# Three products of a chunked linear attention in column tiles of 32, in one stretch on TensorE, with the next unit's key transposes behind them

## The chip, the cores and the metric

One core of one Trainium2 chip runs the whole program. The time is device microseconds from launch to end; lower is better. Beside the timed runs there is one execution taken with the hardware profiler. All rows below are from that one.

## What is computed

A linear attention with a decaying state feeds two MLPs in a row. Four batches, eight heads, 768 steps, head size 48; then 3072 tokens through 384 → 2048 → 384 twice.

```python
for t in range(S):
    cur = np.einsum('bhd,bhe->bhde', u[None] * kt, vt)
    y[:, :, t] = np.einsum('bhd,bhde->bhe', rt, state + cur)
    state = wt[:, :, :, None] * state + np.einsum('bhd,bhe->bhde', kt, vt)
...
h = x @ w_in
g = np.where(h > 0.0, h, alpha * (np.exp(np.minimum(h, 0.0)) - 1.0))
return (g @ w_out).astype(np.float32)      # second MLP: g = h * sigmoid(h)
```

## The kernel before

The steps are cut into six chunks of 128. A **unit** is one chunk of one batch with all eight heads, that is, four pairs of heads; there are 24 units, numbered chunk by chunk (unit n is chunk n // 4 of batch n % 4). The first MLP works on six blocks of four units each. Block 0's units (0 to 3) are computed alone at the start (`dense_units`). From then on the attention of the next four units is woven into the first MLP of the present block: units 4 to 7 into block 0, and so on to units 20 to 23 into block 4. Block 5 and the whole second MLP have no attention beside them.

A block has 16 **slots**, one for each 128 of the 2048 hidden channels. A slot issues nine wide matmuls into `ph` (L447), then nine into `po` (L478) for the slot two before it, and calls `tick` twice, once behind each nine. A tick takes at most one of the six steps `t0` to `t5` of a unit (`round_ticks`), so a unit is spread over some seven ticks. Every engine runs its instructions in program order.

The steps of unit n on TensorE: `scores` (L274 for units below 9, L282 from there on) in t0 and t1, the key transposes `ktok` (L300) in t3, `past` (L345: the state against the decayed queries) and `outer` (L315: keys against values, for the state) in t4, `within` (L365: the masked scores against values) in t5. Around them: `masked` on VectorE (L291), which reads the score buffers; `ktok_copy` on ScalarE (L306), which brings the transposed keys to SBUF for `outer`; `update` (VectorE L325 and L327, then two copies on ScalarE, L329), which brings the product of `outer` into the state; `split` (ScalarE L377 `xh`, then VectorE L378 `xl`), which brings `y`, the sum of `past` and `within`, into the MLP's input. The same steps also prepare unit n + 1 (`do(...)`): decay scans, the products q and k with their decays (`q`, `kt`), the bonus diagonal (`diag`). Units 4 and 8 (`ALONE`) are prepared at the head of their block (`prep_rest`).

`past` writes `y`, 384 rows in three groups of 128 partitions, by seven matmuls 96, 32 or 64 columns wide; `outer` takes two per pair, 64 and 48 wide. `within` already writes tiles of 32 partitions only, four of them after one another on four different column groups. Units 20 to 23 are of the last chunk and have neither transposes nor `outer` nor `update`; units 0 to 3 are of the first and have no `past`.

Scores, transposes, `y`, the product of `outer` and the sums for the diagonal (L229) share three PSUM buffers (`ps_a`, tag `att`). A buffer is free again when the last instruction that reads it is done.

Of the kernel before, what the change touches and what calls it, by code (L numbers as in the profile page):

```python
# [7 lines left out]
F32 = mybir.dt.float32  # L8
# [5 lines left out]
ACTF = mybir.ActivationFunctionType  # L14
# [10 lines left out]
ALONE = (sum(BLOCKS[:1]), sum(BLOCKS[:2]))  # L25
# [9 lines left out]
def kernel(  # L35
# [21 lines left out]
    nc = tc.nc  # L57
    B, H, S, D = r.shape
    NT, DM = out.shape
    DFF = moe_w_out.shape[0]  # L60
    RB = w_ch.shape[2]
    L = 128
    NCH = S // L
    NU = B * NCH
    NP = H // 2
    KT = DM // 128
# [9 lines left out]
    ps_a = ctx.enter_context(tc.tile_pool(name="ps_a", bufs=3, space=PSUM))  # L76
# [4 lines left out]
    ch_p = attn.enter_context(tc.tile_pool(name="ch", bufs=2))  # L81
# [23 lines left out]
    ident = const.tile([128, 128], F32, name="ident")  # L105
# [28 lines left out]
    HALF = (slice(0, 64), slice(64, RB))  # L134
# [17 lines left out]
    def prep_steps(n):  # L152

        st = un[n]
# [87 lines left out]
        def kt():  # L242
            tk = st["kd"] = ch_p.tile([RB, NP, L], F32, tag="tk", name="tk")
            nc.vector.tensor_tensor(out=tk, in0=st["c"][:, 1], in1=k_decay, op=ALU.mult)
            if n >= FIRST_ROUNDED:
                rounding(tk, rounded["kh"], rounded["kl"])

        return dict(scan=scan, scan_back=scan_back, far=far, whole_decay=whole_decay, bonus=bonus, products=products, summed=summed, diag=diag,
                    q=q, kt=kt)


    state = [st_p.tile([RB, NP, 2 * D], F32, name=f"state{b}") for b in range(B)]
# [3 lines left out]
    def pe_steps(n, xt, col, free=None):  # L256
        ch, b = divmod(n, B)
        st = un[n]
        ps = {}

        def ps_att(shape, name):
            if free and name == "sc":
                return free.pop(0).rearrange("p (j t) -> p j t", j=NP)
            return ps_a.tile(shape, F32, tag="att", name=name)


        def scores(h):
            if n < FIRST_ROUNDED:

                if h == 0:  # L270
                    ps["p"] = [ps_att([128, NP, L], "sc") for _ in range(2)]
                for j in (2 * h, 2 * h + 1):
                    for e, rows in enumerate(HALF):
                        nc.tensor.matmul(  # L274
                            ps["p"][e][:, j, :], st["kd"][rows, j, :], st["q"][rows, j, :], start=True, stop=True)
                return
            p = ps["p", h] = ps_att([128, 2, 2, L], "sc")
            terms = [(rounded["k" + a], rounded["q" + b]) for a, b in ("hh", "hl", "lh")]
            for jj in range(2):
                j = 2 * h + jj  # L280
                for i, (a, b) in enumerate(terms):
                    nc.tensor.matmul(  # L282
                        p[:, jj].rearrange("p e t -> p (e t)"), a[:, j, :],
                        b[:, j].rearrange("p e t -> p (e t)"), start=i == 0, stop=i == len(terms) - 1)

        def masked(h):
            if n < FIRST_ROUNDED:
                to, p = st["a"][:, :, h, :], ps["p"][h]
            else:
                to, p = (t.rearrange("p j e t -> p (j e) t") for t in (st["a"][:, 2 * h:2 * h + 2], ps["p", h]))  # L290
            nc.vector.copy_predicated(to, upper.unsqueeze(1).to_broadcast([128, NP, L]), p)  # L291

        last = ch == NCH - 1

        def ktok():
            if last:
                return
            p = ps["kt"] = ps_att([128, NP, RB], "ktp")
            for j in range(NP):
                nc.tensor.transpose(p[:, j, :], st["kd"][:, j, :], ident[0:RB, 0:RB])  # L300

        def ktok_copy():
            if last:
                return
            t = st["kt"] = ch_p.tile([128, NP, RB], F32, tag="kt", name="kt", bufs=1)
            nc.scalar.activation(out=t, in_=ps["kt"], func=ACTF.Copy)  # L306

        def outer():
            if last:
                return  # L310
            p = ps["u"] = ps_att([RB, NP, D], "upd")
            for j in range(NP):

                for e, rows in enumerate(HALF):
                    nc.tensor.matmul(  # L315
                        p[rows, j, :], st["kt"][:, j, rows], st["v"][:, j, 64 * e:64 * e + D],
                        start=True, stop=True)

        def update():
            if last:  # L320
                return
            s, up = packed[b], ps["u"]
            g = st["gl"].to_broadcast([RB, NP, D])
            if ch:
                nc.vector.tensor_tensor(out=s, in0=up, in1=s, op=ALU.add)  # L325
                up = s
            nc.vector.tensor_tensor(out=s, in0=up, in1=g, op=ALU.mult)  # L327
            for e, rows in enumerate(HEAD):
                nc.scalar.activation(out=state[b][rows, :, e * D:(e + 1) * D], in_=s[rows], func=ACTF.Copy)  # L329

        def past():

            y = ps["y"] = ps_att([128, KT, L], "y")
            if not ch:
                return

            for j in range(NP):
                c0 = 2 * D * j
                while c0 < 2 * D * (j + 1):
                    kt, p0 = divmod(c0, 128)  # L340
                    m = min(2 * D * (j + 1) - c0, 128 - p0)
                    if p0 % 64:
                        m = 32
                    c = c0 - 2 * D * j
                    nc.tensor.matmul(  # L345
                        y[p0:p0 + m, kt, :], state[b][:, j, c:c + m], st["q"][:, j, :],
                        start=kt == 0, stop=False, skip_group_check=True)
                    c0 += m

        def within():  # L350
            y = ps["y"]
            vf = st["v"].rearrange("p j c -> p (j c)")
            for step in range(4):
                for base in range(4):


                    todo = []
                    for kt in range(KT):
                        blk = 4 * kt + base
                        j, i = divmod(blk, 3)  # L360
                        ha, hb = (64 + D) * j, (64 + D) * j + 64
                        todo += {0: [(blk, 2 * j, ha)], 1: [(blk, 2 * j, ha + 32), (blk, 2 * j + 1, hb - 16)],
                                 2: [(blk, 2 * j + 1, hb + 16)]}[i]
                    blk, h, c = todo[step]
                    nc.tensor.matmul(  # L365
                        y[32 * base:32 * base + 32, blk // 4, :], vf[:, c:c + 32], st["a"][:, h // 2, h % 2, :],
                        start=not ch and step == 0, stop=step == 3 or todo[step + 1][0] != blk,
                        skip_group_check=True)

        def split():  # L370
            split_x(xt, slice(col, col + L), ps["y"], nc.vector)

        return dict(scores=scores, masked=masked, ktok=ktok, ktok_copy=ktok_copy, outer=outer,
                    update=update, past=past, within=within, split=split)

    def split_x(xt, sl, src, eng):
# [177 lines left out]
    def round_ticks(n):  # L554
        pe, do = round_parts(n)

        def t0():
            pe["scores"](0)
            do("bonus")
            do("products")  # L560
            do("scan")
            load_unit(n + 2, "kr")

        def t1():
            pe["scores"](1)
            do("scan_back")
            do("whole_decay")
            if n + 1 not in ALONE:
                load_unit(n + 3, "w")
            pe["masked"](0)  # L570

        def t2():
            pe["masked"](1)
            do("summed")
            do("far")
            do("q")
            do("diag")

        def t3():
            pe["ktok"]()  # L580
            pe["ktok_copy"]()
            do("kt")
            do("diag", 1)
            if n + 1 not in ALONE:
                load_unit(n + 3, "c")

        def t4():
            pe["past"]()
            pe["outer"]()
            pe["update"]()  # L590

        def t5():
            pe["within"]()
            pe["split"]()
            load_unit(n + 2, "v")

        return [t0, t1, t2, t3, t4, t5]

    def dense_units():

        count = BLOCKS[0]
        prep, pe = {}, {}
# [5 lines left out]
        def begin(n):  # L608
            pe[n], _ = round_parts(n, [banks[3 * (n % 2)], banks[3 * (n % 2) + 1]])
            pe[n]["scores"](0)  # L610
            pe[n]["scores"](1)
            pe[n]["ktok"]()

        def keep_clock(k):
            for _ in range(k):
# [2 lines left out]
        for n in range(-1, count):  # L618
# [33 lines left out]
            if more:  # L652
                w_split()
                w_load()
                if n >= 0:
                    w_scale()
                pe[n + 1]["ktok_copy"]()
                p["diag"](0)
                p["diag"](1)
            if n == -1:  # L660
# [30 lines left out]
    last = None  # L691
# [299 lines left out]
```

## Time and profile before

| | |
|---|---|
| median of 3 timed runs | 966.77 us (966.73 to 966.84) |
| the profiled execution, its own time | 965.98 us |
| its span, first to last instruction | 964.1 us |
| TensorE busy in the span | 940.4 us (98%) |
| VectorE, ScalarE, GpSimd busy | 489.2, 501.4, 133.0 us |
| mean granted TensorE clock | 0.986 of full |
| share of the DMA engines' time, data packets | 22.3% |

A start in a timeline row is in us from the start of the span. TensorE starts matmuls while earlier ones still drain, so what one costs is read from one start to the next, not from its duration.

### The profile page before, as it was taken

What the parts mean: (1) busy time and instruction counts of PE and PEld (TensorE: products, weight loads), DVE (VectorE), ACT (ScalarE), POOL (GpSimd) and SP (SyncE); (2) the same over time, 40 slices, a digit from 0 to 9 for tenths busy, and PEclk for the clock granted to TensorE, in tenths of its full rate; (3) what the DMA queues carried; (4) which work ended last, traced back from release to release, by engine and by line L of the source; (5) the groups of instructions that cost most, each with busy time, mean ns of one, the idle gap of its engine ahead of it and who ended that gap; (6) DMA issues with size and microseconds to landing.
All of it is one profiled execution on the core that took longest, in us unless ns stands there. A gap on an engine that the chain in (4) does not pass through costs nothing.

```text
span 964.1 us, 14152 instructions
## 1 busy us (share of the span) xinstructions
PE 940.4 (98%) x5638; PEld 795.4 (82%) x5638; DVE 489.2 (51%) x726; ACT 501.4 (52%) x901; POOL 133.0 (14%) x101
## 2 busy tenths in 40 slices
PE   7779999999999999999999999999999999999997
PEld 7657777888778888887788889999999999999996
DVE  8789877766666666666357873212212212222111
ACT  6888857465555555465369884323323323333322
POOL 0000013343444333336000000000000000000000
PEclk8789999999999999999999999999999999999999
DMA  8644504211312222120054440010200200200001
GB/s 247 193 148 157 167 29 133 65 56 56 107 56 81 82 63 65 55 78 11 18 179 145 168 146 1 7 60 1 65 2 1 66 1 1 66 1 1 33 0 37
DMA packets 32218, 68.62 MB, mean 71 GB/s; under 512 B 3600, under 2 KB 13968, under 8 KB 32144
## 3 DMA queue, kind: packets, MB, share of 16 engines
q1 hardware_dynamic: 32144, 67.64, 22.3%
q8 instruction: 46, 0.75, 0.3%
q14 instruction: 28, 0.23, 0.1%
HBM read 58.19 MB, written 9.44 MB: 70 GB/s over the span
## 4 chain that ended last, share of the span: by engine, by line
PE 88%; ACT 4%; DVE 4%; issue 1%; ACTq 0%; DVEq 0%
PE ph L447 39%; PE po L486 21%; PE po L478 19%; PE y L345 3%; PE sc L282 2%; PE y L365 2%; ACT am L201 1%; ACT wh L432 1%; PE upd L315 1%; DVE wst L418 1%; ACT wst L409 1%; PE ktp L300 1%; DVE both L160 1%; DVE wst L420 1%; ACT am L178 0%
## 5 line engine op out<-in xcount | busy, mean ns | idle before, releaser
L470 DVE TENSOR_TENSOR gl<-g,gh 128x512 fp32r<-128x512 f32 x192 | 143.1, 745 | 319.7 <-ACT gh L469 318.9
L447 PE MATMUL ph<-xh,wh 128*128 128x512 f32 x576 | 229.6, 399 | 0.0
L447 PE MATMUL ph<-xl,wh 128*128 128x512 f32 x576 | 227.3, 395 | 0.0
L447 PE MATMUL ph<-xh,wl 128*128 128x512 f32 x576 | 227.2, 394 | 0.0
L469 ACT ACTIVATE gh<-g 128x512 fp32r<-128x512 f32 x192 | 120.9, 630 | 153.5 <-PE po L486 109.6
L486 PE MATMUL po<-wh,gl 128*128 128x384 f32 x384 | 129.6, 338 | 0.0
L486 PE MATMUL po<-wh,gh 128*128 128x384 f32 x384 | 129.4, 337 | 0.0
L458 ACT ACTIVATE g<-ph 128x512 f32<-128x512 f32 x96 | 57.3, 597 | 138.1 <-PE ph L447 137.3
L486 PE MATMUL po<-wl,gh 128*128 128x384 f32 x384 | 129.1, 336 | 0.0
L447 PEld LDWEIGHTS ph<-xh,wl 128*128 128x128 f32 x576 | 108.7, 189 | 23.5
L447 PEld LDWEIGHTS ph<-xh,wh 128*128 128x128 f32 x576 | 108.8, 189 | 21.8 <-issue 2.0
L447 PEld LDWEIGHTS ph<-xl,wh 128*128 128x128 f32 x576 | 108.9, 189 | 18.6
L478 PE MATMUL po<-gh,wh 128*128 128x512 f32 x288 | 116.1, 403 | 0.0
L478 PE MATMUL po<-gl,wh 128*128 128x512 f32 x288 | 112.6, 391 | 0.0
L478 PE MATMUL po<-gh,wl 128*128 128x512 f32 x288 | 112.4, 390 | 0.0
L454 ACT ACTIVATE g<-ph 128x512 f32<-128x512 f32 x96 | 56.6, 590 | 69.2 <-PE ph L447 69.1
L463 DVE SCALAR_TENSOR_TENSOR g<-g,ph 128x512 f32<-128x512 f32 x96 | 65.4, 681 | 35.3 <-ACT g L456 34.5
L486 PEld LDWEIGHTS po<-wh,gh 128*128 128x128 f32 x384 | 72.3, 188 | 4.4 <-ACT x2s L497 0.2
L486 PEld LDWEIGHTS po<-wl,gh 128*128 128x128 f32 x384 | 72.1, 188 | 4.0
L486 PEld LDWEIGHTS po<-wh,gl 128*128 128x128 f32 x384 | 72.1, 188 | 0.0
L233 POOL TENSOR_TENSOR ql<-tq,qh 64x512 fp32r<-64x512 f32 (+1 forms) x30 | 42.5, 1416 | 169.9 <-ACT qh L232 168.8
L478 PEld LDWEIGHTS po<-gh,wh 128*128 128x128 f32 x288 | 54.2, 188 | 13.0 <-issue 1.9
(92 smaller groups left out, 1106.6 us busy)
## 6 DMA issues: line engine op xcount, KB each, us to landing
wst<-in_moe_w_in_dram SPq DMA_DIRECT2D x32, 384.0 KB, 3.1
wst<-in_moe_w_out_dram SPq DMA_DIRECT2D x32, 384.0 KB, 3.9
in_c<-in_rk_ch_dram SPq DMA_DIRECT2D x24, 448.0 KB, 4.1
in_w<-in_w_ch_dram SPq DMA_DIRECT2D x24, 226.2 KB, 2.8
in_v<-in_v_tok_dram SPq DMA_DIRECT2D x24, 224.0 KB, 2.7
x_d<-x2s SPq DMA_DIRECT2D x18, 256.0 KB, 2.3
xl<-x_d SPq DMA_DIRECT2D x6, 768.0 KB, 5.2
out_dram<-os SPq DMA_DIRECT2D x24, 192.0 KB, 2.0
```

The lines of the kernel that those rows point to most:

```text
L233: nc.gpsimd.tensor_tensor(out=lo, in0=x, in1=hi.bitcast(F32), op=ALU.subtract)
L282: nc.tensor.matmul(p[:, jj].rearrange("p e t -> p (e t)"), a[:, j, :], b[:, j].rearrange("p e t -> p (e t)"), start=i == 0, stop=i == len( ...
L345: nc.tensor.matmul(y[p0:p0 + m, kt, :], state[b][:, j, c:c + m], st["q"][:, j, :], start=kt == 0, stop=False, skip_group_check=True)
L365: nc.tensor.matmul(y[32 * base:32 * base + 32, blk // 4, :], vf[:, c:c + 32], st["a"][:, h // 2, h % 2, :], start=not ch and step == 0, st ...
L447: nc.tensor.matmul(ph, lhs, xt[rhs][:, kt, 0:nt], start=n == 0, stop=n == 3 * KT - 1)
L454: nc.scalar.activation(out=g, in_=ph, func=ACTF.Exp)
L458: nc.scalar.activation(out=g, in_=ph, func=ACTF.Silu)
L463: nc.vector.scalar_tensor_tensor(out=g, in0=g, scalar=-1.0, in1=ph, op0=ALU.mult, op1=ALU.max)
L469: nc.scalar.activation(out=gh, in_=g, func=ACTF.Copy)
L470: nc.vector.tensor_tensor(out=gl, in0=g, in1=gh.bitcast(F32), op=ALU.subtract)
L478: nc.tensor.matmul(po[ot][:, 0:nt], lhs, rhs, start=f == 0 and i == 0, stop=f == NF - 1 and i == 2)
L486: nc.tensor.matmul(po[t][:, 0:DM], lhs[:, sl], rhs["o", f], start=f == 0 and i == 0, stop=f == NF - 1 and i == 2)
```

## The change

`past` is issued as twelve matmuls of 32 columns, three for each of the four column groups. `outer` is issued as four per pair of heads, 32, 32, 32 and 16 columns wide. Both order them so that four neighbours go to four different column groups, as `within` does. The steps move: t5 now issues `past`, `outer`, `within` and then the key transposes of unit n + 1, one behind the other on TensorE; `update`, `split` and the copy of those transposes follow on the other engines. t4 keeps only the second half of `diag` (which does something for units below 9 alone), t3 only `kt` and a load. Units 4 and 8 have their own transposes and copy in t1, behind the scores.

```diff
-        def ktok():
-            if last:
-                return
-            p = ps["kt"] = ps_att([128, NP, RB], "ktp")
...
+        def ktok():
+            if n // B == NCH - 1:
+                return
+            p = st["ktp"] = ps_a.tile([128, NP, RB], F32, tag="att", name="ktp")
             for j in range(NP):
                 nc.tensor.transpose(p[:, j, :], st["kd"][:, j, :], ident[0:RB, 0:RB])
...
         def outer():
-                for e, rows in enumerate(HALF):
+                for c in range(0, RB, 32):
+                    rows, e = slice(c, min(c + 32, RB)), c // 64
                     nc.tensor.matmul(
                         p[rows, j, :], st["kt"][:, j, rows], st["v"][:, j, 64 * e:64 * e + D],
                         start=True, stop=True)
...
         def past():
-            for j in range(NP):
-                c0 = 2 * D * j
-                while c0 < 2 * D * (j + 1):
-                    kt, p0 = divmod(c0, 128)
-                    m = min(2 * D * (j + 1) - c0, 128 - p0)
-                    if p0 % 64:
-                        m = 32
-                    c = c0 - 2 * D * j
+            for kt in range(KT):
+                for base in range(4):
+                    j, i = divmod(4 * kt + base, 3)
                     nc.tensor.matmul(
-                        y[p0:p0 + m, kt, :], state[b][:, j, c:c + m], st["q"][:, j, :],
+                        y[32 * base:32 * base + 32, kt, :], state[b][:, j, 32 * i:32 * i + 32], st["q"][:, j, :],
                         start=kt == 0, stop=False, skip_group_check=True)
-                    c0 += m
...
         def t1():
             pe["scores"](1)
+            if n in ALONE:
+                own = prep_steps(n)
+                own["ktok"]()
+                own["ktok_copy"]()
...
         def t3():
-            pe["ktok"]()
-            pe["ktok_copy"]()
             do("kt")
-            do("diag", 1)
             if n + 1 not in ALONE:
                 load_unit(n + 3, "c")
         def t4():
+            do("diag", 1)
+        def t5():
             pe["past"]()
             pe["outer"]()
+            pe["within"]()
+            do("ktok")
             pe["update"]()
-        def t5():
-            pe["within"]()
             pe["split"]()
+            do("ktok_copy")
             load_unit(n + 2, "v")
```

`dense_units` calls the same transposes and copy under their new names at the same places.

## Rows read from the trace of the kernel before

**Rows 1.** The page: busy us (share of the span) and count of the engines.
```profile
PE 940.4 (98%) x5638; PEld 795.4 (82%) x5638; DVE 489.2 (51%) x726; ACT 501.4 (52%) x901; POOL 133.0 (14%) x101
```

**Rows 2.** Windows (start, blocks 0, 1, 4): length, busy PE PEld DVE ACT POOL, PEclk, DMA.
```profile
0.00:35.00 35.00, 27.57 (x288) 24.22 (x288) 29.41 (x51) 25.29 (x63) 1.74 (x9) 0.78 0.74 221
...
40.90:140.30 99.40, 91.57 (x632) 69.51 (x632) 85.18 (x126) 80.97 (x153) 4.21 (x4) 0.97 0.42 136
140.30:228.30 88.00, 88.00 (x613) 70.18 (x613) 61.56 (x94) 52.19 (x102) 34.97 (x24) 1.00 0.28 82
...
401.90:489.00 87.10, 87.10 (x537) 69.40 (x536) 47.10 (x71) 42.12 (x72) 23.79 (x16) 1.00 0.17 55
```

**Rows 3.** Waits of the weight-load engine, 150 to 480 us: total, times, longest.
```profile
PEld y L345 <- issue: 9.1, 48, 0.2
...
PEld po L478 <- ACT g L454: 0.4, 2, 0.2
```

**Rows 4.** Timeline of TensorE, unit 10: start, duration, instruction, count.
```profile
194.59 0.55 PE L300 MATMUL ktp<-ident,tk 112*128 112x112 f32 x4
194.91 0.47 PE L447 MATMUL ph<-xh,wh 128*128 128x512 f32 x1
195.22 0.39 PE L447 MATMUL ph<-xl,wh 128*128 128x512 f32 x1
...
197.06 1.68 PE L345 MATMUL y<-tq,state 112*96 112x128 f32 x13
...
199.48 0.40 PE L478 MATMUL po<-gl,wh 128*128 128x512 f32 x1
...
201.09 0.39 PE L478 MATMUL po<-gh,wl 128*128 128x512 f32 x1
201.41 1.08 PE L365 MATMUL y<-am,in_v 128*32 128x128 f32 x32
202.42 0.50 PE L447 MATMUL ph<-xh,wh 128*128 128x512 f32 x1
202.76 0.40 PE L447 MATMUL ph<-xl,wh 128*128 128x512 f32 x1
```

**Rows 5.** Timeline of TensorE, unit 20 (last chunk).
```profile
415.64 1.79 PE L345 MATMUL y<-tq,state 112*96 112x128 f32 x14
...
417.70 0.39 PE L447 MATMUL ph<-xl,wh 128*128 128x512 f32 x1
```

**Rows 6.** Lines L315 and L365, whole run: count, duration min/median/max in ns.
```profile
L315 PE MATMUL upd<-in_v,kt x320: 206/222/340, 12.8 to 392.2; 128*64 128x48 f32 x93, 128*48 128x48 f32 x67
...
L365 PE MATMUL y<-am,in_v x768: 272/273/424, 17.4 to 479.1; 128*32 128x128 f32 x192
```

**Rows 7.** Waits of the weight-load engine, whole run, on masks and on the key copy.
```profile
PEld ktp L300 <- DVE am L291: 4.3, 3, 3.1
...
PEld upd L315 <- ACT kt L306: 1.3, 3, 0.8
```

**Rows 8.** Timeline of block 0: transposes of unit 4; unit 4's split, unit 5's scores.
```profile
60.77 1.01 PE L300 MATMUL ktp<-ident,tk 112*128 112x112 f32 x4 [2.64 <-DVE am L291]
...
72.22 0.56 DVE L378 TENSOR_TENSOR xl<-y,xh 128x384 fp32r<-128x384 f32 x1 [0.52 <-ACT xh L377]
...
72.35 0.71 PE L274 MATMUL sc<-tq,tk 64*128 64x128 f32 x8
```

**Rows 9.** Timeline of block 0: unit 6's update and split, unit 7's scores.
```profile
111.44 0.36 DVE L327 TENSOR_TENSOR packed<-packed,whole 112x192 f32<-112x192 f32 x1
...
111.89 0.74 ACT L329 ACTIVATE state<-packed 48x192 f32<-48x192 f32 x2 [1.26 <-PE y L365]
...
114.06 0.71 PE L274 MATMUL sc<-tq,tk 64*128 64x128 f32 x7
...
115.11 0.47 ACT L377 ACTIVATE xh<-y 128x384 fp32r<-128x384 f32 x1
...
115.61 0.56 DVE L378 TENSOR_TENSOR xl<-y,xh 128x384 fp32r<-128x384 f32 x1 [0.48 <-ACT xh L377]
```

More of the change, by code (lines that the diff above doesn't have):

```diff
@@ L246, in kt, with ktok_copy @@
                 rounding(tk, rounded["kh"], rounded["kl"])
-        return dict(scan=scan, scan_back=scan_back, far=far, whole_decay=whole_decay, bonus=bonus, products=products, summed=summed, diag=diag,
+        def ktok():
+            if n // B == NCH - 1:
+                return
+            p = st["ktp"] = ps_a.tile([128, NP, RB], F32, tag="att", name="ktp")
+            for j in range(NP):
+                nc.tensor.transpose(p[:, j, :], st["kd"][:, j, :], ident[0:RB, 0:RB])
+        def ktok_copy():
+            if n // B == NCH - 1:
+                return
+            t = st["kt"] = ch_p.tile([128, NP, RB], F32, tag="kt", name="kt", bufs=1)
+            nc.scalar.activation(out=t, in_=st["ktp"], func=ACTF.Copy)
+        return dict(ktok=ktok, ktok_copy=ktok_copy, scan=scan, scan_back=scan_back, far=far, whole_decay=whole_decay, bonus=bonus, products=products, summed=summed, diag=diag,
                     q=q, kt=kt)
@@ L293, in pe_steps @@
         last = ch == NCH - 1
-        def ktok():
-            if last:
-                return
-            p = ps["kt"] = ps_att([128, NP, RB], "ktp")
-            for j in range(NP):
[L300 to L306, printed above, removed]
         def outer():
@@ L335, in past @@
                 return
-            for j in range(NP):
-                c0 = 2 * D * j
-                while c0 < 2 * D * (j + 1):
-                    kt, p0 = divmod(c0, 128)
-                    m = min(2 * D * (j + 1) - c0, 128 - p0)
-                    if p0 % 64:
-                        m = 32
-                    c = c0 - 2 * D * j
+            for kt in range(KT):
+                for base in range(4):
+                    j, i = divmod(4 * kt + base, 3)
                     nc.tensor.matmul(
-                        y[p0:p0 + m, kt, :], state[b][:, j, c:c + m], st["q"][:, j, :],
+                        y[32 * base:32 * base + 32, kt, :], state[b][:, j, 32 * i:32 * i + 32], st["q"][:, j, :],
                         start=kt == 0, stop=False, skip_group_check=True)
-                    c0 += m
         def within():
@@ L371, in split @@
             split_x(xt, slice(col, col + L), ps["y"], nc.vector)
-        return dict(scores=scores, masked=masked, ktok=ktok, ktok_copy=ktok_copy, outer=outer,
+        return dict(scores=scores, masked=masked, outer=outer,
                     update=update, past=past, within=within, split=split)
@@ L611, in begin @@
             pe[n]["scores"](1)
-            pe[n]["ktok"]()
+            prep[n]["ktok"]()
         def keep_clock(k):
@@ L656, in dense_units @@
                     w_scale()
-                pe[n + 1]["ktok_copy"]()
+                p["ktok_copy"]()
                 p["diag"](0)
```

## The prediction

> **What bounds the kernel now.** First the engines on the page: TensorE is busy 98% of the span, the next engine half of it [rows 1]. Then the same in windows, one for each block, because a mean over stages with different limits says little: in blocks 1 to 4 TensorE is busy from end to end at a granted clock of 1.00 (2.4 GHz), VectorE 54 to 70% of the time; in block 0 TensorE lacks 8 us and VectorE is busy 85 of 99 [rows 2]. Then who waited: between 150 and 480 us the weight-load engine's longest wait is for nothing but "issue", 48 pauses of 0.2 us in front of `past`, while a wait on another engine comes to 0.4 us in all [rows 3]. So in blocks 1 to 4 the program is TensorE's own list of instructions, and what is taken from it comes off the end; after block 4 nothing is changed and everything moves forward with it. Block 0 is different: there the waits on masks and on the key copy stand in the list too [rows 7].
>
> **What a unit's steps cost on TensorE today.** From the start of a step to the start of the second wide matmul behind it, less one wide step, plus what the step's own start came late. A wide step is 0.23 us (199.48 to 201.09 is seven of them) [rows 4]. The second wide matmul is taken since the first one is started early and then drawn out.
> - Transposes: 194.59 to 195.22, less 0.23: 0.40 us.
> - `past` and `outer`: 197.06 to 199.48, less 0.23: 2.19 us.
> - `within`: 201.41 to 202.76, less 0.23, plus 0.09 for a start 0.32 instead of 0.23 behind its neighbour: 1.21 us.
>
> Together 3.80 us a unit [rows 4]. In the last chunk `past` alone is 415.64 to 417.70, less 0.23: 1.83 us, and `past` with `within` 3.04 us [rows 5].
>
> **How tiles of 32 run.** `within` is 16 matmuls, and the trace has 32 records, so each is two passes. 32 passes take 1.08 us from first start to last end; one takes 0.273, so the last begins 0.81 us behind the first: eight steps of four passes, 0.115 us from step to step [rows 4, 6]. Four column groups run side by side. Were they one after another, 31 steps would each be 0.026 us, shorter than any matmul here. `past` today is 14 passes that begin over some 1.5 us (1.79 long less 0.27), 0.12 each, hardly better than one by one, with a 0.2 us pause at changes of width [rows 3, 5].
>
> **The new run, step by step.** `past` becomes 12 matmuls, 24 passes, three matmuls for each column group: six steps of four passes. It streams 128 columns like `within`, so I take 0.115 a step; that it uses 112 rows instead of 128 I cost at nothing, since today's `past`, with 112 too, begins a pass every 0.12 us with its pauses included. `outer` becomes 16 matmuls, 32 passes, eight steps. No row has tiles of 32 with 48 streamed columns. Bounds: below, a pass with 48 columns takes 0.206 us at least where one with 128 takes 0.273 [rows 6], so a step is 0.115 − 0.067 = 0.048 and eight are 0.38; above, 32 passes at `within`'s mean of 0.026 are 0.84. I take 0.38, because `within` shows that the four groups do not wait for each other. `within` stays at eight steps.
>
> From the last wide matmul in front: 0.32 to the first small one; (6 + 8) × 0.115 + 0.38 = 1.99 for the steps, less one, since the last step's start counts: 1.88; 0.20 to the next full-width matmul, as between 202.22 and 202.42; transposes 0.32 to the wide one behind, then 0.31 to the second [rows 4]. That is 3.03, less two wide steps of 0.23: **2.57 us** against 3.80. A unit gains 1.23 us. Units 8 to 19 are twelve: 14.8 us. (Unit 8's own transposes in t1 cost the 0.40 that they cost today.) In the last chunk: 0.32 + 14 × 0.115 − 0.115 + 0.20 + 0.34 − 0.46 = 1.90 against 3.04, 1.14 a unit, 4.6 us for four.
>
> **What is moved and hidden.** In blocks 1 to 4 `update`, `split` and the key copy come behind the run on VectorE and ScalarE. The work is the same, one tick later or earlier; VectorE is idle a third of the time there [rows 2]. No transfer is moved past another on SP's queue, and nothing of GpSimd's is moved. The key copy gets a whole unit (some 20 us) of lead before `outer` reads it, where today it has one tick. New is a wait: the three PSUM buffers are handed out in the order in which they came free. (That fits today's trace: unit 4's transposes start 0.06 us behind the first mask of its scores [rows 8], and unit 5's scores start while `xl` still reads `y` [rows 8], so they don't use that buffer.) Today the next unit's scores get the buffers of the key copy and of `outer`; after the change those of `outer` and of `y`. For units from 9 on the second is wanted by t1 only, a tick (2 us of wide matmuls) later than t0; I cost it at nothing. If that cover failed, scores and the wide matmuls queued behind them would stand. For units below 9 t0 wants both at once, and that is block 0.
>
> **Block 0.** Gains: three units' worth before the last such wait, and 4.3 + 1.3 us of waits on masks and the key copy [rows 7], which fall away since transposes no longer follow the masks. But unit n + 1's scores now wait for unit n's `xl`, and `xl` hangs on VectorE, whose own list is nearly full there, and comes later in it: the update's two operations (0.36 each) and the two state copies (0.74 together) now stand right in front of `xh` (0.47) and `xl` (0.56) [rows 9]. Unit 7's scores start at 114.06 today, unit 6's `xl` ends at 116.17 [rows 9]. If `xl` ends as today, the scores are 2.1 us later than now; if all 1.46 us are added, 3.6. I take 2.8. Whatever was won earlier in the block is lost in that wait (unit 5's scores, at 72.35 with `xl` ending at 72.78 [rows 8], lose it once before). Behind it unit 7's own run gains 1.23 and a wait of about 0.3 goes. So block 0 is 1.2 us **slower**. Bounds: 3.5 slower, if the delays add up in VectorE's list; 5 faster, half of 4 × 1.23 + 5.6, if the scores do not wait. Unit 4 has one wait more: the sums for unit 5's diagonal now take the buffer that its key copy has just left, about 1 us, and that too is lost in the wait of unit 5's scores. Units 0 to 3, computed alone, only change `outer`, by 0.46 us each at most; TensorE lacks 7.4 of 35 us there [rows 2], so I count nothing.
>
> **The sum.** 14.8 + 4.6 − 1.2 = 18.2 us. The profiled execution's 965.98 becomes 947.8; it lies 0.8 below the median of the timed runs, 966.77, so the median becomes **948.6**. A measurement of this kernel can tell about 0.2%, 1.9 us, from no change.
>
> **The rivals.**
> 1. *The narrow passes of `outer` are paid one by one.* Twice as many instructions with the same 48 columns: if each pass has a fixed price that column groups can't share, eight steps become 32 × 0.026 = 0.84 instead of 0.38, 0.46 a unit, 5.5 us in twelve units: 954.1. For it: no row shows 48 columns in tiles of 32. Against: the starts in `within`. The Trainium skill speaks for this rival (TensorEngine Tiling (Array Packing), Instruction Overhead): about 60 cycles for each matmul, so that a short one costs as much as one of 60 columns, and one shouldn't tile a dimension that is already small; 60 cycles at 2.4 GHz would be an estimated 25 ns a pass, 0.80 us a unit, and no row here decides it.
> 2. *Block 0 gains too*, because the scores find another buffer or VectorE moves up: 5 us faster instead of 1.2 slower, 942.4. Against it: VectorE's 85 of 99 us [rows 2].
> 3. *Slower: TensorE's sequencer can't feed the run.* Today's longest burst of small passes is 32 at 0.026 us [rows 4]; the new one has 88, each with its weight load. Per pass x the run costs 87x + 0.09 + 0.20 + 0.32 + 0.31 − 0.23 = 87x + 0.69, which is today's 3.80 at x = 0.036. At 0.045 a unit costs 4.60, 0.80 more, twelve units 9.6; the last chunk still gains a little (55 × 0.045 + 0.40 = 2.9 against 3.04, 0.6 in all): with block 0's 1.2, 977.0. For it: what the queue held beforehand may have carried `within`. Against it: the 14 passes of `past` and 16 of `outer` in one row show no pause but those at changes of width.
>
> **How the numbers follow.** Forecast 0.67; rival 1 0.13; rival 2 0.10; rival 3 0.05; 0.05 for less than any of these, around no change. The likeliest is 948.6, by itself 945.5 to 951.5 (block 0's bounds and a tenth of a step either way). The range takes in rivals 1 and 2: 942.4 to 955.0. Faster by over 0.2%: 0.92; same 0.03; slower 0.05.
>
> **What would show it.** In the timeline of unit 10 `past`, `outer`, `within`, transposes in one piece of some 2.5 us with no pause of 0.2 us inside it; if rival 1 holds, `outer` takes 0.8 of it. The pauses for issue in front of L345 fall from 48 to one a unit. Blocks 1 to 3 shorter by 4.9 us each, block 4 by 4.6, block 0 about as long, with waits of scores on L378 in place of those on masks. Wrong would be blocks 1 to 3 that shrink by less than 2 us, or waits of TensorE on VectorE there.

## The result and the profile after

The changed kernel takes **949.62 us**, the median of four runs (947.38 to 950.46), against 966.81 for the kernel before: a ratio of 0.982 (95% interval 0.980 to 0.984), 17.2 us less. The forecast was 948.6, 18.2 less. The profiled execution is the fastest of the four: 947.38, with a span of 945.6; from profile to profile 18.6 us went.

The page of the changed kernel (busy us, share of the span, count of instructions), to be set beside [rows 1]:

```profile
PE 918.1 (97%) x6158; PEld 790.8 (84%) x6158; DVE 489.4 (52%) x726; ACT 502.4 (53%) x901; POOL 133.9 (14%) x101
```

TensorE issues 520 matmuls more and is busy 22.3 us less. The other engines do what they did, to a microsecond.

Where the time went, block by block. The windows run from the first wide step of one block to that of the next, but for block 0's, which begins with its second slot; so they add up to everything from there on. The second slot starts at 45.93 us before and at 45.99 after. (The last window of [rows 2] ran 3.5 us past the end of block 4; only a share was read from it.) Columns: window, length, busy us (count) of PE, PEld, DVE, ACT and POOL, PEclk, DMA share, GB/s. The kernel before, blocks 0 to 4 and the rest:

```profile
45.93:140.34 94.41, 88.44 (x616) 67.04 (x615) 81.22 (x120) 77.25 (x147) 4.21 (x4) 0.96 0.42 137
140.34:228.33 87.99, 87.99 (x613) 70.17 (x612) 61.55 (x94) 52.19 (x102) 34.97 (x24) 1.00 0.28 82
228.33:315.12 86.79, 86.79 (x602) 69.83 (x600) 55.87 (x86) 48.45 (x90) 34.15 (x24) 1.00 0.24 70
315.12:401.90 86.78, 86.78 (x601) 69.83 (x600) 55.83 (x86) 48.23 (x89) 34.14 (x24) 1.00 0.24 71
401.90:485.53 83.63, 83.63 (x521) 66.51 (x520) 46.26 (x70) 40.29 (x69) 23.79 (x16) 1.00 0.15 49
485.53:964.13 478.60, 471.65 (x2325) 421.59 (x2323) 151.93 (x214) 202.43 (x325) 0.00 (x0) 1.00 0.14 47
```

The changed kernel, the same six windows:

```profile
45.99:141.58 95.59, 85.46 (x719) 67.40 (x719) 80.70 (x120) 78.19 (x147) 4.15 (x4) 0.95 0.41 135
141.58:224.78 83.20, 83.20 (x721) 68.92 (x720) 60.31 (x94) 52.53 (x103) 35.04 (x24) 1.00 0.29 87
224.78:306.43 81.65, 81.65 (x705) 68.22 (x704) 56.38 (x85) 48.34 (x90) 34.45 (x24) 1.00 0.25 75
306.43:387.73 81.30, 81.30 (x701) 67.88 (x700) 56.92 (x85) 47.48 (x89) 34.43 (x24) 1.00 0.25 76
387.73:466.72 78.99, 78.99 (x561) 65.38 (x560) 46.58 (x70) 40.71 (x70) 24.07 (x16) 1.00 0.16 51
466.72:945.61 478.89, 471.62 (x2325) 421.36 (x2323) 152.02 (x214) 202.60 (x325) 0.00 (x0) 0.99 0.14 47
```

Blocks 1 to 4 are shorter by 4.79, 5.14, 5.48 and 4.64 us, the rest is longer by 0.29, and block 0 is longer by 1.18. In blocks 1 to 4 TensorE is still busy from end to end, so each microsecond taken from its list came off the end. In block 0 it is busy 3.0 us less and the block is longer all the same: it waits 4.2 us more than before.

The run itself: timeline of TensorE in the changed kernel at unit 10, then at unit 20 in the last chunk (start, duration, instruction, count), beside [rows 4, 5]:

```profile
197.46 0.39 PE L474 MATMUL po<-gh,wl 128*128 128x512 f32 x1
197.78 0.86 PE L342 MATMUL y<-tq,state 112*32 112x128 f32 x24
198.46 0.52 PE L316 MATMUL upd<-in_v,kt 128*32 128x48 f32 x32
198.80 1.06 PE L361 MATMUL y<-am,in_v 128*32 128x128 f32 x32
199.80 0.60 PE L253 MATMUL ktp<-ident,tk 112*128 112x112 f32 x4
200.17 0.48 PE L443 MATMUL ph<-xh,wh 128*128 128x512 f32 x1
200.48 0.39 PE L443 MATMUL ph<-xl,wh 128*128 128x512 f32 x1
...
403.28 0.39 PE L443 MATMUL ph<-xh,wl 128*128 128x512 f32 x1
403.60 0.86 PE L342 MATMUL y<-tq,state 112*32 112x128 f32 x24
...
405.61 0.40 PE L474 MATMUL po<-gl,wh 128*128 128x512 f32 x1
```

From the start of the last wide step in front to that of the second behind, less two wide steps of 0.228: 200.48 − 197.46 − 0.46 = 2.56 us at unit 10 (2.57 on average over the eleven runs with transposes in blocks 1 to 3), where the four pieces took 3.80; and 405.61 − 403.28 − 0.46 = 1.87 at unit 20, where it was 3.04.

Waits of the weight-load engine in the changed kernel, 150 to 462 us (total, times, longest), beside [rows 3]:

```profile
PEld y L342 <- issue: 5.6, 16, 0.4
```

One pause in front of each of the 16 runs instead of 48; a further 10 of 0.2 us stand in front of transposes, at the change from 32 columns to 128. These are pauses of the weight loads; the matmul engine itself has no wait in blocks 1 to 4, before or after.

Block 0, waits of the matmul engine in the changed kernel, 46 to 141 us (total, times, longest). The waits on masks of [rows 7] are gone, and scores wait in their place. The last line is from the kernel before, 46 to 141 us:

```profile
PE sc L287 <- DVE tk L244: 3.5, 1, 3.5
PE sc L287 <- ACT kt L259: 2.9, 2, 1.7
PE ph L443 <- DVE g L459: 2.1, 1, 2.1
PE sc L287 <- DVE packed L326: 1.5, 1, 1.5
...
PE sc L274 <- DVE tk L244: 2.2, 1, 2.2
```

The first of these waits is not for a buffer: at the head of the block unit 4's scores wait for that unit's own keys (`tk`), as they do in the kernel before. New are the scores' waits for the key copy and for the update, 4.4 us in three, and one of 2.1 us of wide matmuls for `g` (VectorE L459).

And where two of them arise, the timeline at the turn from unit 4 to unit 5 in the changed kernel (in brackets: idle time before it, and what ended it); the last line is the same turn from unit 6 to unit 7:

```profile
70.75 0.49 PE L287 MATMUL sc<-tq,tk 64*128 64x128 f32 x2 [1.51 <-DVE packed L326]
71.19 0.75 ACT L330 ACTIVATE state<-packed 48x192 f32<-48x192 f32 x2 [0.45 <-DVE packed L328]
71.96 0.49 ACT L373 ACTIVATE xh<-y 128x384 fp32r<-128x384 f32 x1
72.35 0.54 ACT L259 ACTIVATE kt<-ktp 128x448 f32<-128x448 f32 x1
...
72.94 0.84 PE L287 MATMUL sc<-tq,tk 48*128 48x128 f32 x6 [1.70 <-ACT kt L259]
...
117.22 0.71 PE L287 MATMUL sc<-tq,tk 48*128 48x128 f32 x6 [1.25 <-ACT kt L259]
```

Unit 5's scores need two PSUM buffers at once. The first comes free when the update (L326) has read `upd`, the second when ScalarE has copied the transposed keys of unit 5, which is its fourth operation behind the update. In the order of release that follows from the change, that copy gives the buffer; e5 below is the test of this.

### The profile page after: what moved, and what is told of

Same layout as the page of the kernel before. It is cut to its first block, busy times and chain, and to the rows that moved or that the text cites. A ratio compares the mean times of both kernels' runs of the same rounds, so it can differ in the third digit from the quotient of the medians.

```text
span 945.6 us, 15205 instructions
## 1 busy us (share of the span) xinstructions
PE 918.1 (97%) x6158; PEld 790.8 (84%) x6158; DVE 489.4 (52%) x726; ACT 502.4 (53%) x901; POOL 133.9 (14%) x101
## 4 chain that ended last, share of the span: by engine, by line
PE 89%; DVE 6%; DMA 2%; ACT 2%; issue 1%; SPq 0%; DVEq 0%; ACTq 0%
PE ph L443 40%; PE po L482 21%; PE po L474 19%; PE sc L295 2%; PE y L361 2%; PE y L342 1%; DVE wst L414 1%; PE ktp L253 1%; DVE wl L429 1%; DVE wst L416 1%; DMA in_v<-in_v_tok_dram 1%; DVE am L304 1%; DVE gl L466 1%; PE upd L316 1%; DMA above_sb<-in_above_dram 1%
## 5 line engine op out<-in xcount | busy, mean ns | idle before, releaser
L465 ACT ACTIVATE gh<-g 128x512 fp32r<-128x512 f32 x192 | 120.8, 629 | 153.7 <-PE po L482 109.7
L450 ACT ACTIVATE g<-ph 128x512 f32<-128x512 f32 x96 | 56.5, 589 | 52.2 <-PE ph L443 52.1
L459 DVE SCALAR_TENSOR_TENSOR g<-g,ph 128x512 f32<-128x512 f32 x96 | 65.4, 681 | 27.7 <-ACT g L452 27.1
```

Of the source, the lines that this page charges most:

```text
L450: nc.scalar.activation(out=g, in_=ph, func=ACTF.Exp)
L459: nc.vector.scalar_tensor_tensor(out=g, in0=g, scalar=-1.0, in1=ph, op0=ALU.mult, op1=ALU.max)
L465: nc.scalar.activation(out=gh, in_=g, func=ACTF.Copy)
```

## The experiments

A unit's cost on TensorE is taken in all of them as above: from wide step to wide step, less the wide steps. "Block 0" is the window as above.

### Widths alone, and order alone

**e1_tiles_only** keeps the narrow tiles and puts every step back where it was. The diff shows what the edit amounts to; the own transposes of units 4 and 8 leave t1 for t3 as well.

```diff
         def t3():
+            own = prep_steps(n)
+            own["ktok"]()
+            own["ktok_copy"]()
             do("kt")
+            do("diag", 1)
...
         def t4():
-            do("diag", 1)
+            pe["past"]()
+            pe["outer"]()
+            pe["update"]()
         def t5():
-            pe["past"]()
-            pe["outer"]()
             pe["within"]()
-            do("ktok")
-            pe["update"]()
             pe["split"]()
-            do("ktok_copy")
```

> Only the narrow tiles; every step at its old place. My account (tiles and order each have a price of their own): past and outer together cost 0.09 for the start + 0.69 + 0.38 - 0.05 of steps + 0.20 + 0.34 - 0.23 for the return to full width = 1.42 us instead of 2.19, so 0.77 a unit for units 4 to 19 and 0.85 a unit in the last chunk, and block 0 gains too, because nothing new waits there: 16 x 0.77 + 4 x 0.85 = 15.7, that is 951.1 us. If the one run is what counts, and narrow tiles with a return to full width behind each step bring little: some 960 us.

Measured: 953.19 us (952.77 to 954.07), ratio 0.987 (0.985 to 0.989). Timeline of TensorE around unit 10 in this kernel:

```profile
195.78 0.40 PE L443 MATMUL ph<-xh,wl 128*128 128x512 f32 x1
196.10 0.86 PE L342 MATMUL y<-tq,state 112*32 112x128 f32 x24
...
197.57 0.40 PE L474 MATMUL po<-gl,wh 128*128 128x512 f32 x1
```

`past` and `outer` cost 197.57 − 195.78 − 0.46 = 1.33 us, 0.85 less than before. `past` alone in the last chunk costs 0.99 where it was 1.83. Blocks 1 to 4 take 85.21, 83.57, 83.57 and 80.35 us, 12.5 less together, but block 0 takes 94.19, only 0.22 less than before, though the four runs there are 3.4 us shorter. What they save there waits for the key copy (4.0 us in four waits of L316) and for the masks (2.9 us in three).

**e2_order_only** keeps the new order and puts the old loops of `past` and `outer` back.

```diff
         def outer():
-                for c in range(0, RB, 32):
-                    rows, e = slice(c, min(c + 32, RB)), c // 64
+                for e, rows in enumerate(HALF):
...
         def past():
-            for kt in range(KT):
-                for base in range(4):
-                    j, i = divmod(4 * kt + base, 3)
+            for j in range(NP):
+                c0 = 2 * D * j
+                while c0 < 2 * D * (j + 1):
...
```

> Only the new order, past and outer as wide as before the change. My account: one return to full width less a unit, some 0.24 us x 12 and 0.2 us x 4, less the waits of block 0 (about 2 us): 965 us, hardly to be told from before. If the one run is what counts: 955 us or less.

Measured: 965.37 us (964.02 to 966.32, ten runs), ratio 0.9995 (0.9986 to 1.0005): no difference. The run is 3.55 us instead of 3.80, the last chunk's 2.84 instead of 3.04; blocks 1 to 4 give 4.3 us together. Block 0 takes 96.42, 2.0 more, and the medians differ by 0.5 us only. So the order by itself brings little that reaches the end, and the widths carry most of the result: 12.7 of some 17 us. The two do not simply add up: 12.5 and 4.3 us in blocks 1 to 4 are 16.8, where both together gave 20.05. One stretch saves 0.25 us a unit with the old widths (3.80 to 3.55), and 0.38 with the narrow ones (1.33 + 0.40 + 1.21 = 2.94 to 2.57).

### The price of a narrow pass

**e3_outer_wide** is the changed kernel with `outer` in its old widths.

```diff
-                for c in range(0, RB, 32):
-                    rows, e = slice(c, min(c + 32, RB)), c // 64
+                for e, rows in enumerate(HALF):
```

> The changed kernel with outer in tiles of 64 and 48 columns again. My account: two changes of tile width inside the run (0.20 instead of 0.115 each) and eight steps of 0.056 instead of 0.048: 0.26 to 0.47 us more a unit in twelve units, 3.1 to 5.6 us slower than the changed kernel, 952.7 to 955.2. If narrow tiles don't pay for 48 streamed columns (each pass has a fixed price): the same as the changed kernel or faster, 949.6 or less.

Measured: 952.27 us (951.48 to 952.54), ratio 0.986 (0.984 to 0.987). Timeline of TensorE, unit 10 of this kernel:

```profile
199.64 0.86 PE L341 MATMUL y<-tq,state 112*32 112x128 f32 x24
200.43 0.67 PE L315 MATMUL upd<-in_v,kt 128*64 128x48 f32 x16
201.02 1.08 PE L360 MATMUL y<-am,in_v 128*32 128x128 f32 x32
```

`outer` in 16 wider passes takes 201.02 − 200.43 = 0.59 us, where 32 narrow ones take 198.80 − 198.46 = 0.34; and `past` in front of it takes 0.79 instead of 0.68, where the tile now changes its width. The whole run is 2.95 us on average against 2.57, and blocks 1 to 3 are 1.52 us longer each, 4.6 together, as expected (3.1 to 5.6). The medians differ by 2.7 only, as the changed kernel's block 0 varies from run to run (next section). Rival 1, by which 32 narrow passes would cost 0.84, falls: with half as many passes `outer` costs more, not less. The Trainium skill's rule that was set beside it (TensorEngine Tiling (Array Packing), Instruction Overhead: about 60 cycles for each matmul) would have given an estimated 0.80 us; the measured 0.34 is 0.011 us a pass, less than half of that price, so the trace does not agree where four column groups run side by side. That estimate counts the 32 passes of the trace; counted for the kernel's 16 calls it would be 0.40, and the measured time is below that too.

### What block 0 loses, and to whom

**e0_changed_again** is the changed kernel once more, measured together with e5, e6 and e7 below, and **e4_block0_old_places** is the edit of e1 for units below 8 alone (the changed order from unit 8 on).

```diff
...
         def t4():
-            do("diag", 1)
+            if n < 8:
+                pe["past"]()
+                pe["outer"]()
+                pe["update"]()
+            else:
+                do("diag", 1)
...
```

> The changed kernel once more, beside the next three, for its spread (947.4 to 950.5 in four runs). If its runs differ by how long the scores wait in block 0: another profile has blocks 1 to 4 to 0.1 us as the first one (83.2, 81.7, 81.3, 79.0) and differs in block 0 alone (95.6 from the second slot on).

> Narrow tiles everywhere, the new order for units from 8 on, the old places of all steps for units 4 to 7 in block 0. If block 0's loss is the scores' wait for buffers that the update and the key copy free late: that wait is gone, block 0 gains 4 x 0.77 = 3.1 us on before instead of losing 1.2, 945.3 us. If VectorE's full list bounds block 0 whatever TensorE does: no change from the changed kernel, 949.6.

Measured: e0 949.41 us (947.83 to 950.99), ratio 0.983 (0.981 to 0.985); e4 945.77 (945.32 to 946.34), 0.979 (0.977 to 0.981). Block 0 takes 94.26 in e4. That is 1.3 to 2.9 us less than in the two profiles of the changed kernel, which its order loses there; but the old order, with the narrow tiles, is not faster there than the kernel before (94.41): as in e1, its `outer` waits for the key copy, 4.0 us in four waits. So e4's time is near the first forecast (945.3) without its reason: block 0 gained 0.15 us on before, not 3.1.

The second profile of the changed kernel also shows where its runs differ. Blocks 1 to 4 are the same to 0.01 us (83.20, 81.65, 81.30, 78.99); block 0 is this (columns as in the windows above):

```profile
47.14:144.28 97.14, 88.34 (x720) 68.95 (x719) 80.79 (x120) 78.50 (x147) 3.88 (x4) 0.91 0.40 133
```

97.14 at a granted clock of 0.91, against 95.59 at 0.95. TensorE is idle for less time (8.8 us against 10.1) but busy 2.9 us longer: it is the clock behind the waits that differs, not the waits. Unit 7's scores, for example, wait 1.25 us for the key copy in the first profile and 1.22 in the second; from 119.5 to 123.0 us, behind that wait, the granted clock is 1.00 in the first and 0.51 in the second.

**e5_copy_first** moves one line: the key copy is issued ahead of update and split.

```diff
             do("ktok")
+            do("ktok_copy")
             pe["update"]()
             pe["split"]()
-            do("ktok_copy")
```

> The changed kernel with the key copy ahead of update and split in program order. If the scores of units 5 and 7 wait for the key copy behind the state copies on ScalarE (they waited 1.70 and 1.25 us for it, after 1.51 for the update): those 3 us go, 946.6. If VectorE's list sets block 0's end anyway: no change, 949.6.

Measured: 944.83 us (943.65 to 945.86), ratio 0.978 (0.977 to 0.980), 4.6 below e0 on the same chip. Timeline of this kernel at the same turn, unit 4 to unit 5:

```profile
71.61 0.52 ACT L259 ACTIVATE kt<-ktp 128x448 f32<-128x448 f32 x1
71.73 1.17 PE L287 MATMUL sc<-tq,tk 64*128 64x128 f32 x8 [1.09 <-DVE packed L326]
```

The copy now runs beside the update, and the scores wait for one buffer alone, that of the update (2.1 us in two waits over the block, against 4.4 in three for both). Block 0 takes 92.52. The run in blocks 1 to 3 is as it was (2.55). So it is the place of the copy in ScalarE's list that held the second buffer.

### VectorE's list, or the order?

Two edits were to tell whether the waits of block 0 come from VectorE's full list or from the chain itself. **e6_pool_wl** (the changed kernel) and **e7_old_places_pool_wl** (e4) move 13 subtractions of 0.96 us from VectorE to GpSimd, which does little in block 0.

```diff
-            nc.vector.tensor_tensor(out=l, in0=t, in1=h.bitcast(F32), op=ALU.subtract)
+            (nc.gpsimd if m == 0 and f >= 3 else nc.vector).tensor_tensor(
+                out=l, in0=t, in1=h.bitcast(F32), op=ALU.subtract)
```

> The changed kernel with 13 of the 16 subtractions that split the first MLP's weights (0.96 us each on VectorE, in block 0) on GpSimd, which is idle there. If VectorE's full list bounds block 0: 12.5 us come off it and most of the waits of the scores go, block 0 some 4 to 8 us shorter, 942 to 946. If order and buffers bound it: less than 1 us.

> Narrow tiles, old places in block 0 (945.8 before), and the same 13 subtractions on GpSimd. If VectorE's list is what kept block 0 from the 3.1 us that the narrow tiles save there: 938 to 942. If not: 945 to 946.

Measured: e6 955.94 us (955.05 to 956.23), ratio 0.990 (0.988 to 0.991); e7 954.01 (951.9 to 955.81), 0.988 (0.987 to 0.990). Both are slower than without the edit. Line `gl` of VectorE in block 0 (count, duration min/median/max in ns, from and to), first in the changed kernel, then in e6, and then two neighbours in e6's timeline:

```profile
L466 DVE TENSOR_TENSOR gl<-g,gh x15: 673/684/693, 53.6 to 138.4; 128x512 fp32r<-128x512 f32 x15
```

```profile
L467 DVE TENSOR_TENSOR gl<-g,gh x15: 659/1930/1987, 52.8 to 147.2; 128x512 fp32r<-128x512 f32 x15
```

```profile
67.01 1.87 POOL L429 TENSOR_TENSOR wl<-wst,wh 128x768 fp32r<-128x768 f32 x1 [4.70 <-ACT wh L428]
67.49 1.95 DVE L467 TENSOR_TENSOR gl<-g,gh 128x512 fp32r<-128x512 f32 x1 [0.35 <-ACT gh L466]
```

VectorE has 13 instructions fewer and is busy 86.8 us instead of 80.7. Its own subtraction lasts from 67.49 to 69.44, that is until GpSimd is done at 68.88 and then 0.56, about what it takes alone. The load was not taken from VectorE but made larger, so neither theory is tested. The Trainium skill says this beforehand (SBUF — State Buffer, Who interferes with whom): a VectorE instruction with two inputs in SBUF contends with a GpSimd instruction that reads SBUF, and the later one stands until the other is done. The trace agrees, 0.68 to 1.93 us.

So the load was shortened instead: **e8_short_joins** (the changed kernel) and **e10_before_short_joins** (the kernel before) join only 96 of 768 columns in 13 of the 16 weight pieces, which takes some 17 us off VectorE's list in block 0 and leaves its order alone. The other columns of these weights stay unjoined, so these two kernels do not do the whole work.

```diff
             m, f, st = scaled.pop(0)
-            low, t = st[:, :, 0], st[:, :, 1]
+            n = 96 if m == 0 and f >= 3 else 2 * DM
+            low, t = st[:, 0:n, 0], st[:, 0:n, 1]
```

> The changed kernel with the two operations of VectorE that join the halves of the first MLP's weights, 0.96 us each, on 96 of 768 columns in 13 of 16 pieces (the other columns of these weights stay unjoined): some 20 us less on VectorE in block 0, with nothing added elsewhere. If VectorE's full list is what makes the scores wait and keeps block 0 from its gain: block 0 some 9 to 12 us shorter, 937 to 941. If the buffers' order alone does it, the waits stay: 946 or more.

> The kernel before with the same short joins. If VectorE's list is what costs block 0 its waits on masks and key copies (5.6 us and the clock behind them): 957 to 960, and the changed kernel with short joins is 19 to 21 us faster than this one, since block 0 then pays out its 4 x 1.23 us too. If block 0 can't gain for another reason: the difference stays at 16 to 17 us.

Measured: e8 942.58 us (941.09 to 943.51), ratio 0.975 (0.974 to 0.977); e10 960.83 (960.38 to 961.28), 0.995 (0.993 to 0.996). Windows of block 0, e8 and then e10:

```profile
46.95:137.71 90.76, 86.15 (x720) 68.23 (x720) 63.17 (x120) 77.40 (x147) 3.87 (x4) 0.92 0.43 142
```

```profile
45.88:135.48 89.60, 86.33 (x615) 66.47 (x615) 63.76 (x120) 76.77 (x147) 4.16 (x4) 0.98 0.44 143
```

In e10 the waits on masks and on the key copy are gone: VectorE's list made them. Block 0 is 4.8 us shorter, of which 2.7 are idle time of TensorE and 2.1 busy time, at a granted clock of 0.98 instead of 0.96. In e8 block 0 also falls by 4.8, not by the 9 to 12 that the list alone was to give, and scores still wait for the key copy, though VectorE is now busy 63 of 91 us. Waits of the matmul engine in e8, and its timeline at that turn:

```profile
PE sc L287 <- ACT kt L259: 2.9, 2, 1.7
```

```profile
70.97 0.71 PE L287 MATMUL sc<-tq,tk 48*128 48x128 f32 x6 [1.27 <-ACT kt L259]
```

2.9 us in two waits, as with the full list. So this wait belongs to the order: update, state copies, `xh`, key copy, one after another, do not fit into the tick between the run and the next scores. The difference of the two kernels, 18.25 us, lies between what the two theories gave (16 to 17, and 19 to 21) and decides for neither. The windows say more. The new order makes block 0 longer by 1.18 us with the full list (95.59 against 94.41) and by 1.16 with the short one (90.76 against 89.60). So in these profiles the list costs 4.8 us and the order 1.2, each whatever the other is, and block 0 does not pay out its narrow tiles with the short list either. With the changed kernel's second profile (97.14) the same differences from it would be 6.4 and 2.7 us, so how exactly the two add stays open.

### Two more tries at block 0

**e9_block0_two_runs** takes e5 and splits the run for units below 8: past, outer and update in t4, the rest in t5.

```diff
         def t4():
             do("diag", 1)
+            if n < 8:
+                pe["past"]()
+                pe["outer"]()
+                pe["update"]()
...
```

> The changed kernel with the key copy first (944.8 as it is) and, in block 0 alone, past, outer and update one tick earlier than within, transposes, copy and split. If what is left of block 0's waits is the scores' wait for the update (1.5 and 1.2 us in the last look): it goes, against 0.3 us a unit for a second run: 943 to 944. If VectorE's list bounds block 0 either way: 944 to 946.

Measured: 948.66 us (947.71 to 950.42), ratio 0.983 (0.981 to 0.984), a miss. Scores wait 6.0 us in two waits for the key copy: with the update a tick earlier, the state copies stand ahead of the key copy again in ScalarE's list, and between the two comes other work of ScalarE (L405 and L407 at one turn, L428, L465, L450 and L452 at the other).

**e11_copy_first_scores_late** takes e5 and gives the scores of units below 9 one tick more.

```diff
         def t0():
...
-            pe["scores"](0)
+            if n >= FIRST_ROUNDED:
+                pe["scores"](0)
         def t1():
+            if n < FIRST_ROUNDED:
+                pe["scores"](0)
             pe["scores"](1)
```

> The changed kernel with the key copy first, and the first half of the scores of units 4 to 8 one tick later, in t1 with the second half. If what block 0 still loses is the tick that is missing between the run and the next unit's scores: the waits for the update (2.1 us) and the slow clock behind them go, 942 to 943. If VectorE's list bounds block 0 anyhow, the wait turns up elsewhere: 944 to 946.

Measured: **943.15 us** (942.18 to 944.84, five runs), ratio 0.976 (0.975 to 0.978): the fastest of the kernels that do the whole work, 23 us under the kernel before, though its runs overlap with e5's. Waits of the matmul engine in its block 0:

```profile
PE sc L287 <- DVE tk L244: 3.4, 1, 3.4
PE ph L443 <- DVE g L459: 2.6, 2, 2.1
PE sums L229 <- DVE seed L159: 1.9, 2, 1.0
PE po L474 <- DVE gl L466: 1.0, 1, 1.0
```

The scores' one wait is unit 4's for its own keys, at the head of the block; no scores wait for a buffer any more. What is left is all on VectorE, and block 0, 92.39 us, is hardly shorter than in e5 (92.52): the wait turned up elsewhere, as the second forecast had it, though the time is nearer the first one's. That VectorE's full list makes these waits is likely from e10, but was not tried with this order.

## Why the prediction was right, point by point

- **TensorE's list bounds blocks 1 to 4.** Right: its idle time there is zero in both kernels, and the gain per block is the gain per unit times four. By the terms of the sum, blocks 1 to 4 give 14.8 + 4.6 = 19.4 us; measured 20.05. The first block gives less (unit 8's own transposes stay in t1, where they cost 0.35) and the third more (no transposes stand behind unit 19, and its run takes 2.21): with 1.23 a unit that makes 4.57, 4.92 and 5.27, and each of the three windows lies some 0.2 above it. Where these 0.2 come from was not taken apart. Two figures of the reading were too small, without harm: [rows 3] leaves out 16 pauses of the weight loads in front of `within` (for issue, 5.6 us, up to 0.4 each), and their waits on other engines come to 0.6 us instead of 0.4.
- **The run.** 2.57 foretold, 2.57 measured, and the steps inside it too: `past` 0.68 for 6 × 0.115 = 0.69, `outer` 0.34 for 0.38, the last chunk 1.87 for 1.90. The choice of the lower bound for `outer` was the one that mattered (5.5 us), and it rested on the starts of `within`: four passes at a time. `outer` came out 0.04 below that bound, and the transposes 0.05 above their 0.32 (199.80 to 200.17); that the two cancel is luck, of a small size. That 112 rows instead of 128 cost nothing held.
- **Rival 3**, a sequencer that can't feed 88 passes: the run has no pause among its 88 narrow passes, the steps of 0.115 included. It falls.
- **Block 0.** 1.2 us slower foretold, 1.18 measured in the profiled execution and 2.7 in the second one. The course was right: unit 7's scores come late (their second part starts at 117.22, where all of them started at 114.06; 2.8 us were foretold) and a part is won back behind them. The releaser was not: the prediction gave the second buffer to `xl`, and the waits of scores on L378 that were to show it do not appear; e5 shows that it is the key copy, which in the list stands right behind `xh`. Both end within 0.2 us of each other (72.48 + 0.56 and 72.35 + 0.54), so the sum could not tell them apart; the remedy could, 4.6 us for one moved line. The copy was thought of as work with a unit of lead, which holds in blocks 1 to 4; its other role, as what gives the buffer back, was left out. Nor did the sum have the 2.1 us for `g` or the clock, so that 1.2 became 1.18, and not 2.7, is in part luck. Rival 2 (block 0 gains 5 us) is false for this kernel; e5 and e11, with 92.52 and 92.39 against 94.41, have 2 us of it.
- **What was not foretold.** That TensorE's clock falls behind these waits (next section but one), and that block 0 spreads the runs over 3.1 us, where the four of the kernel before beside them agreed within 0.3 (later sets of 7 to 13 runs of it spread by 1.6 to 2.1). The forecast was made for a profiled execution, and that one is at the fast end of the spread (18.6 less, 18.2 foretold). That the median is 1.0 us above the forecast for this reason is argued, not shown.

## What to carry to other kernels

Before a matmul with few columns is called too small to tile further, look at the starts inside a burst that is already tiled: if four neighbours start together, the price is that of a step of four, and one width throughout can be cheaper than fewer, wider passes, as here. When steps are moved, list what each moved instruction gives back (a buffer of a pool that is handed out in order of release) as well as what it computes; the copy of the keys was early as data and late as a buffer. And an order that is free in one stage is to be costed again in a stage where the next step wants the buffers a tick earlier, as the scores of units below 9 do.

## What the runs showed of the hardware that was not expected

- **A pass in a tile of 32 with 48 streamed columns costs 0.011 us** when four column groups take turns: 32 in 0.34 us, where the 24 of `past` with 128 columns take 0.68.
- **The clock behind a wait.** Windows of the changed kernel over and behind the scores' waits of 1.51 and 1.70 us, and then two wide steps from the second of them (columns as in the windows and timelines above):

```profile
70.70:74.30 3.60, 1.85 (x9) 1.34 (x10) 1.38 (x4) 3.08 (x8) 0.00 (x0) 0.87 0.55 158
74.30:76.70 2.40, 2.40 (x7) 1.92 (x6) 2.36 (x5) 2.37 (x5) 0.00 (x0) 0.50 0.33 72
```

```profile
74.30 0.63 PE L474 MATMUL po<-gl,wh 128*128 128x512 f32 x1
74.73 0.63 PE L474 MATMUL po<-gh,wl 128*128 128x512 f32 x1
```

The granted clock is 0.50, the lower level of 1.2 GHz, for these 2.4 us behind the waits, with TensorE busy all the time; ahead of them (66.0 to 70.7) and from 76.7 on it is 1.00 and 0.99; a wide step takes 0.43 us instead of 0.23 there. So the two waits cost at least some 1.2 us more than their own length, and it happens once more each behind the waits that end at 51.74 and at 107.05. It is not so behind every wait (unit 7's scores above), and the kernel before has such stretches in block 0 too: 0.59 from 46 to 50 us, 0.53 from 60.5 to 64.

- **VectorE and GpSimd exclude each other** in these subtractions (e6: VectorE's takes 1.93 us instead of 0.68 beside GpSimd's of 1.88), so GpSimd's idle time in block 0 could not be used for this work.
